# Buffers of the front, and the order of the step behind an out block, in a gated mix of two attention branches

## The chip, the cores and the metric

The kernel runs on one core of one Trainium2 chip. The metric is the device time of one execution in microseconds (us). The core has five engines that run side by side and meet by semaphores: PE (TensorE, the matmuls), DVE (VectorE), ACT (ScalarE), POOL (GpSimd) and SP (SyncE, which here only issues DMAs). Each engine takes its instructions strictly in the order of the program, so an instruction that waits holds up all behind it on that engine. PE's results land in PSUM, of which there are eight banks of 128 x 512 floats.

## The reference, cut to what matters

The input x has 2048 rows of 512. Two attention branches of 32 heads of 16 are computed from it and mixed row by row by a gate.

```python
# branch A: each query sees 8 keys, at distances 0, 2, ..., 14 behind it
qkv = x @ wqkv;  logits = einsum("bhsd,bhswd->bhsw", q, kg) * scale
o_a = einsum("bhsw,bhswd->bhsd", softmax(logits), vg);  a = o_a @ wo_a
# branch B: 32 query heads, one key head and one value head, all 2048 keys
q = x @ wq;  k = x @ wk;  v = x @ wv
o_b = einsum("bhqk,bkd->bhqd", softmax(q k^T * scale), v);  b = o_b @ wo_b
g = sigmoid((x * gate_w).sum(-1, keepdims=True))
return g * a + (1 - g) * b
```

Products that feed the softmax or the output are made from two parts (a rounded part and the rest), three matmuls for one, so that float precision is kept.

## The kernel before, in words

**Two phases.** The front makes all projections; the main loop computes branch B and, beside it on POOL, branch A. A planner written in Python runs while the program is built. It keeps estimated clocks of PE, ACT and DVE (`clk`) and times at which each PSUM bank becomes free (`free`), and from these it decides which instruction comes next. What it decides is fixed in the program: on the chip each engine follows that order and waits where the estimate was short.

**The front** (`front_stream`, up to about 285 us). PE computes 14 query projections and then 64 projections for branch A ("lumps"), each of 12 products with 64-row halves of the array, into four banks `pf` in turn. ACT copies each finished bank away.

- A query lump is copied to `qraw` (`queries_post`, line 223). POOL then rounds it to `qhi` and takes the rest as `qlo` (lines 230 and 231), and SP stores both in DRAM. There is one `qraw`, so the copy of a query waits until POOL has ended line 231 for the query before it.
- A lump of branch A is copied to one half of `stage` (`a_post`, line 257); after every second lump SP stores the buffer in DRAM (`ad`, line 265). There are two such buffers, used in turn, so a copy into a buffer waits until the store of two pairs earlier has landed. SP issues these stores in one queue with the query stores and with rows of eight small transfers each (`qst` from `ml`, line 459).

**Fills.** Branch B's softmax needs the largest score of each query. It comes from 2048 extra score matmuls ("fills") with 62-row halves, which the planner puts wherever PE has room: single ones into bank `ps` or `po` (line 328, DVE reduces 128 x 512, line 362), pairs into the two banks `pm` (DVE reduces 128 x 1024, line 350), or as differences: the difference of two key blocks goes to a bank `pd` (line 399), ACT applies Relu and copies it to `dd` (line 411), a second fill and one DVE operation (line 423) give the maximum of both.

**The main loop** has 512 steps, 16 tiles of keys for each of 32 units of queries. A step s has two score pairs, `exp_pair(s, 0)` and `exp_pair(s, 1)` (PE line 471, into the double banks `e0` and `e1`, named `pe` in the profile), each followed by one exponential on ACT (line 477, 128 x 1024), and `weighted(s - 1)`, eight matmuls of the values with the exponentials of the step before into bank `po` (line 486). Between them stand "m2" (a pair of fills into `pm`, if the bank is free within a slack) and "m1" (a single fill into `ps`).

**Out blocks.** Three times, at the first step of a unit, the step is an out block (`out_phase`, `stream`): the output rows of four tiles are computed by 96 products (line 803), each as an upper and a lower half. It uses `e0` and `e1` in turn; `pm` is given up and becomes the two difference banks `pd`. Near its end the planner calls the block "closing" and starts no more differences; once the scores of pair 0 are issued and both `pd` are free it makes `pm` out of them again (`rejoin`) and issues `exp_pair(s, 1)` into `pm`. The last result is taken from `e1` by ACT (line 685) and, behind it, DVE (line 686). The position of the first two blocks is fixed by a step number; the third comes at the first unit's end at which the fills are less than `LEAD` = 1.75 units ahead. The step behind a block has an order of its own. In the order of the step before the change,

```python
        if s - 1 in led:
            order = (0, "m2", "m1", "po", 1)
```

"po" is `weighted(s - 1)`, which needs bank `po` empty of the block's last fill, and both exponentials of the block's step.

**POOL** is busy with branch A (`a_scores`, `a_values`), in its own order; there `av` (line 605) is a scratch tile and `tr4` (line 554) another of the same size.

Of the kernel before, what the change touches and what calls it, by code (L numbers as in the profile page):

```python
# [6 lines left out]
F32 = mybir.dt.float32  # L7
# [6 lines left out]
P = 128  # L14
# [3 lines left out]
DH = 16  # L18
NJ = S // P
C = D // P  # L20
# [9 lines left out]
AG = 2  # L30
# [10 lines left out]
NH = NJ // 2  # L41
LEAD, M2S, M1S, MARGIN = 1.75, 0.5, 0.3, 0.12
# [6 lines left out]
def gated_mix_kernel(ctx, tc, xt, wa, wk, wq, wo_a, wo_b, out):  # L49
# [48 lines left out]
    dd2 = p1.tile([P, 2, 512], F32, name="dd2")  # L98
    wqh = p0.tile([P, C, D], F32R, name="wqh")
    wql = p0.tile([P, C, D], F32R, name="wql")  # L100
    wkr = p0.tile([P, C, P], F32, name="wkr")
    wqr = [t[:, k].rearrange("p (c q) -> p c q", c=C) for t in (wq01, dd) for k in range(2)]
    waraw, wah, wal = {}, {}, {}
    GO = [0, GN + VN, 2 * GN + VN, 3 * GN + VN]
# [112 lines left out]
    def queries_post(m, bank, key, ups_at):  # L217

        nonlocal pool
        settle("rest", 0)  # L220
        own = p0q.tile([P, 512], F32, name="qraw", bufs=1)
        hi, lo = parts_of()
        got = nc.scalar.activation(own, bank, AF.Copy)
        at = after("act", clk["pe"] + T_LAT, 0.62)
        mark(got, at, ups_at)
        free[key] = at + 0.1

        def rest():
            nonlocal pool
            nc.gpsimd.tensor_copy(hi, own)  # L230
            nc.gpsimd.tensor_sub(lo, own, hi.bitcast(F32))
            pool = max(pool, 1e3 * at) + 2300
            queries_out(m, hi, lo)
            if m > 4 and m % 2 and len(stacked) < NB:
                stack(len(stacked))

        tasks.append((max(pool / 1e3, at), rest, (), "rest"))
# [8 lines left out]
    def a_post(gg, j, bank, key, ups_at):  # L246

        if j % 2 == 0:
            settle("store", 1)
            if len(stages) < 2 or "next" in stage:  # L250
                stages.append((stage.pop("next", None) or p1).tile([P, GC, 2, AN], F32, name=f"stage{len(stages)}"))
            stage["t"] = stages[turns[1] % len(stages)]
            turns[1] += 1
        st = stage["t"]
        end = gg == C - 1 and j == NJ - 1
        src = bank[:, :GN].rearrange("p (g n) -> p g n", g=GC)
        got = nc.vector.tensor_copy(st[:, :, 1, :], src) if end else nc.scalar.activation(st[:, :, j % 2, :], src, AF.Copy)
        if gg == 0:
            nc.scalar.activation(vst[:, j, 0:DH + 1], bank[:, GN:GN + DH + 1], AF.Copy)
        at = after("dve" if end else "act", clk["pe"] + T_LAT, 0.5 if gg else 0.7)  # L260
        mark(got, at, ups_at)
        free[key] = at + 0.1
        if j % 2 == 1:
            dst = ad[gg * GC:(gg + 1) * GC, HALO:, :].rearrange("g (p j) n -> p g (j n)", j=NJ)
            tasks.append((at + 0.3, lambda: nc.sync.dma_start(dst[:, :, (j - 1) * AN:(j + 1) * AN], st.rearrange("p g j n -> p g (j n)")), (), "store"))
        if j == NJ - 1:
            tasks.append((at + 1.0, whole, (gg,)))
# [327 lines left out]
    def a_values(g, hf):  # L595
        lg, e = alog.pop(g), aext.pop(g)
        js = slice(NH * hf, NH * hf + NH)
        lgv = lg.rearrange("p w j h -> p w (j h)")
        nc.gpsimd.tensor_mul(asum[g], asum[g], gate[:, 0, js].unsqueeze(2).to_broadcast([P, NH, AG]))
        nc.gpsimd.tensor_mul(lgv, lgv, asum.pop(g).rearrange("p j h -> p (j h)").unsqueeze(1).to_broadcast([P, W, NH * AG]))  # L600
        yield 850
        ao = oa[g // 8][:, js, g % 8 * AC:(g % 8 + 1) * AC].rearrange("p j (h d) -> p j h d", d=DH)
        for w in range(W):
            o = HALO - DIL * w
            av = p2[0].tile([P, NH, AG, DH], F32, name="av", bufs=1) if w else ao
            nc.gpsimd.tensor_mul(av, e[:, o:o + NH, 2 * AC:].rearrange("p j (h d) -> p j h d", d=DH), lg[:, w].unsqueeze(3).to_broadcast([P, NH, AG, DH]))  # L606
            yield 730
            if w:
                nc.gpsimd.tensor_add(ao, ao, av)  # L609
                yield 830  # L610
# [130 lines left out]
    def stream(seq, mm, done, s):  # L741

        nonlocal pp2
        at, told = [0, 0], 0
        ready = free.pop("m2")
        pp2.release()
        pp2 = tc.alloc_tile_pool(name="parts", bufs=1, space=PSUM)
        if len(held[0]) < 2:
            more = p1x[0].tile([P, 2, 512], F32, name="dd2", tag="qx", bufs=1)
            for b in range(2):  # L750
                held[b].append(more[:, b])
                read_d[b].append(0.0)
        apart[:] = [pp2.tile([P, 512], F32, name=f"pd{k}") for k in range(2)]
        free["d0"] = free["d1"] = ready
        free["po"] = 1e9
        cl = [clk["pe"]] * 2
        while min(at) < len(seq) or any(pend):
            if free["po"] > 1e8 and min(at) > 3 and max(cl) > exped[s - 1] + 0.1:
                clk["pe"] = max(cl)
                weighted(s - 1)  # L760
                finish_a((s - 1) // NJ, nc.gpsimd)
                free["po"] = clk["dve"] + 0.1
                cl = [clk["pe"]] * 2
            if apart and max(at) > len(seq) - 6 and s in exped and max(free["d0"], free["d1"]) <= max(cl):
                clk["pe"] = max(cl)
                rejoin()
                exp_pair(s, 1, m2, "m2")
                cl = [clk["pe"]] * 2
            b = int(cl[1] < cl[0])
            clk["pe"] = cl[b]  # L770
            do = side_fill(b, max(at) > len(seq) - 6)
            if do:
                do()
                cl[b] += T_R
            elif at[b] < len(seq) and at[b] <= at[1 - b] + 2:
                dur = mm(b, seq[at[b]])
                cl[b] = clk["pe"] + dur
                at[b] += 1
            else:
                cl[b] += 0.07  # L780
            clk["pe"] = cl[b]
            while told < min(at):
                told += 1
                done(seq[told - 1])
        plain_todo()
        clk["pe"] = max(cl)
        if apart:
            rejoin()
            exp_pair(s, 1, m2, "m2")
# [469 lines left out]
    for s in range(NS + 1):  # L1259
        u, kt = divmod(s, NJ)  # L1260
        if len(stacked) < NU and s >= max(2, 16 * (gone(len(stacked)) + 1)):
            stack(len(stacked))
        if s < NS and kt == 0 and u not in shifted:
            while u not in shifted:
                clk["pe"] += 0.5
                run_tasks()
                if u not in shifted and left.get(u, 1):
                    assert pause(4)
        v = min(x[0][0] for x in (half, slots, [(NU,)]) if x)
        need = left.get(v, NF // NU)  # L1270
        steps = 16 * v - 6 - s
        short = need - 2.8 * max(0, steps) if v < NU else 0
        lead = (NF - to_go()) / 64 - s / 16
        order = (0, "m2", "m1", 1) if s > 1 else (1, "m2", "m1", 0) if s else ()
        if s - 1 in led:
            order = (0, "m2", "m1", "po", 1)
        k, n = outs // 4, C - (outs >= NJ - 4)
        if outs == NJ - 4:
            if short > 0 and steps < 2:
                pause(short)  # L1280
        elif due or outs < NJ and outs // NH in done and kt == 15 and NHG * (k + 1) - 1 in shaped and (lead < LEAD or s >= 16 * (NHG * (k + 2) + 1) - 1):
            if not due:
                prepare(outs, n)
                due.append(n)
            else:
                out_phase(list(range(outs, outs + 4)), due.pop(), s)
                outs += 4
                led.add(s)
                order = ()
        elif short > 0 and steps < 2:  # L1290
            pause(short)

        for which in order:
            if which == "m2":
                if slots or half:
                    fill_ready("m2", M2S)
                else:
                    next(tail, None)
            elif which == "m1":
                if singles(s) and fill_ready("m1", M1S):  # L1300
                    owing[0] -= 1.0
            elif which == "po":
                weighted(s - 1)
            elif s < NS:
                exp_pair(s, which)
        if s - 1 in exped:
            weighted(s - 1)
            if kt == 0 and s < NS:
                finish_a(u - 1, nc.gpsimd)
        run_tasks()  # L1310
        run_pool()
# [79 lines left out]
```

## Time and profile before

| | us |
|---|---|
| median of 3 runs | 1464.12 (1463.6 to 1466.82) |
| the profiled execution | 1463.92 |
| its span, first to last instruction | 1462.1 |
| PE busy in the span | 1448.2 (99%) |
| ACT busy | 1292.0 (88%) |
| DVE busy | 1141.9 (78%) |
| POOL busy | 954.6 (65%) |

The profiled execution is 1.8 us longer than its span; that rest lies outside the first and last instruction. In the rows of the timeline the first number is the start in us from the span's start, the second the duration; then engine, line, operation, what it writes and reads, and how many follow each other (xN). Square brackets hold the idle time of that engine just before, and whose end ended it. In a row of waits the three numbers are us in total, times, and the longest. In a row of windows stand the stretch, its length, the busy time of each engine with the number of its instructions, and PEclk, the share of full clock that TensorE was granted. Line numbers are those of the kernel before.

### The profile page before, as it was taken

Reading aid. Unit: us, or ns where it says so; the run is one execution under the profiler, and the core shown is the slowest. Engines: PE = TensorE matmul, PEld = TensorE weight load, DVE = VectorE, ACT = ScalarE, POOL = GpSimd, SP = SyncE. Lnnn points to the kernel's source line nnn. Section 1 sums busy time; section 2 is a strip of 40 time slices with the busy share of each in tenths; the row PEclk is TensorE's granted clock in tenths of the full one; section 3 lists DMA queues with packets and bytes.
Section 4 is the critical chain, followed back from the end, with each engine's and each line's share of the span. In section 5 each row is a group of like instructions: output and inputs, shape, how many; then the busy total and the mean of one; then the engine's idle time right before and its main releaser. Section 6 shows DMA issues by size and latency. Waiting matters only on the chain.

```text
span 1462.1 us, 29622 instructions
## 1 busy us (share of the span) xinstructions
PE 1448.2 (99%) x10989; PEld 743.1 (51%) x10989; DVE 1141.9 (78%) x1857; ACT 1292.0 (88%) x1649; POOL 954.6 (65%) x1714
## 2 busy tenths in 40 slices
PE   9999999999999999999999999999999999999999
PEld 6899999833333333333333373333333743373335
DVE  6888888788887888888888876888888778778821
ACT  5788888699999999999999988999999889879994
POOL 6951888888979898898898897888881211130000
PEclk9999999999999999999999999999999999999999
DMA  6652442411202111012022020211200000000000
GB/s 225 171 159 72 146 129 89 136 49 41 79 12 79 47 44 68 31 39 78 17 74 72 13 93 8 82 42 42 71 12 13 27 16 1 2 31 1 1 2 29
DMA packets 45688, 85.70 MB, mean 59 GB/s; under 512 B 10400, under 2 KB 28248, under 8 KB 41448
## 3 DMA queue, kind: packets, MB, share of 16 engines
q1 hardware_dynamic: 38552, 45.21, 10.0%
q0 software_dynamic: 6560, 37.95, 7.8%
q8 instruction: 86, 1.41, 0.4%
q10 hardware_dynamic: 432, 0.66, 0.1%
q14 instruction: 58, 0.48, 0.1%
HBM read 57.97 MB, written 25.25 MB: 57 GB/s over the span
## 4 chain that ended last, share of the span: by engine, by line
PE 92%; POOL 2%; ACT 2%; DVE 1%; issue 1%; DMA 1%; SPq 0%; POOLq 0%; ACTq 0%; DVEq 0%
PE po L486 34%; PE pe L471 24%; PE pf L1109 9%; PE pm L328 8%; PE ps L328 5%; PE pe L803 5%; PE pd L399 3%; PE po L328 1%; PE pe L1320 1%; ACT pexp L477 1%; DMA ad<-stage 1%; POOL xl L82 1%; DVE mx L350 1%; DMA xraw<-xt 0%; PE pf L195 0%
## 5 line engine op out<-in xcount | busy, mean ns | idle before, releaser
L477 ACT ACTIVATE pexp<-pe 128x1024 f32<-128x1024 f32 x1021 | 983.4, 1023 | 64.4 <-PE pe L471 61.1
L350 DVE TENSOR_REDUCE mx<-pm 128x2 f32<-128x1024 f32 x470 | 574.0, 1221 | 178.1 <-PE pm L328 174.4
L486 PE MATMUL po<-pexp,vst 128*32 128x512 f32 x4096 | 546.4, 605 | 4.5 <-DVE mx L423 3.3
L471 PE MATMUL pe<-qst,kst 64*128 64x512 f32 x1914 | 492.6, 459 | 2.0 <-ACT pexp L477 2.0
L471 PEld LDWEIGHTS pe<-qst,kst 64*128 64x128 f32 x1914 | 193.5, 184 | 437.0 <-ACT pexp L477 408.6
L411 ACT ACTIVATE dd<-pd 128x512 f32<-128x512 f32 x384 | 224.5, 601 | 50.7 <-PE pd L399 24.7
L362 DVE TENSOR_REDUCE mx<-ps 128x1 f32<-128x512 f32 x309 | 209.8, 679 | 3.4 <-PE pe L803 2.0
L328 PE MATMUL ps<-kst,qst 62*128 62x512 f32 x475 | 194.2, 409 | 0.2
L549 POOL TENSOR_TENSOR pr<-aext 128x256 f32<-128x256 f32 x256 | 181.9, 740 | 4.2 <-DMA aext<-ad 4.0
L328 PE MATMUL pm<-kst,qst 62*128 62x512 f32 x880 | 178.7, 397 | 0.5 <-ACT pexp L477 0.2
L609 POOL TENSOR_TENSOR oa<-oa,av 128x256 f32<-128x256 f32 x224 | 164.1, 733 | 15.8
L486 PEld LDWEIGHTS po<-pexp,vst 128*32 128x32 f32 x4096 | 80.6, 108 | 171.7 <-issue 157.2
L423 DVE CUSTOM_DVE_ANT_0 dd<-ps,dd 128x512 f32<-128x512 f32 x193 | 133.0, 689 | 25.8 <-PE ps L328 7.8
L423 DVE CUSTOM_DVE_ANT_0 dd<-po,dd 128x512 f32<-128x512 f32 x191 | 131.6, 689 | 22.6 <-PE po L328 10.2
L1109 PE MATMUL pf<-wal,xh 64*128 64x384 f32 (+1 forms) x496 | 148.3, 337 | 0.0
L399 PE MATMUL pd<-kd,qst 62*128 62x512 f32 x372 | 146.4, 398 | 1.7 <-ACT dd L411 1.7
L606 POOL TENSOR_TENSOR av<-aext,lg 128x256 f32<-128x256 f32 x224 | 139.4, 622 | 12.6
L1109 PE MATMUL pf<-wah,xh 64*128 64x384 f32 (+1 forms) x496 | 145.7, 338 | 0.0
L1109 PE MATMUL pf<-wah,xl 64*128 64x384 f32 (+1 forms) x496 | 142.3, 337 | 0.0
L328 PEld LDWEIGHTS ps<-kst,qst 62*128 62x128 f32 x475 | 87.8, 185 | 33.7 <-DVE mx L362 25.6
L513 POOL TENSOR_TENSOR rl<-rl,gate_t 128x16 f32<-128x16 f32 x31 | 7.1, 230 | 143.3 <-DVE rl L506 143.1
L1109 PEld LDWEIGHTS pf<-wal,xh 64*128 64x128 f32 x496 | 90.7, 186 | 0.3
(210 smaller groups left out, 1817.6 us busy)
## 6 DMA issues: line engine op xcount, KB each, us to landing
aext<-ad POOLq DMA_DIRECT2D x32, 1056.0 KB, 5.4
ad<-stage SPq DMA_DIRECT2D x32, 384.0 KB
qst<-qd SPq DMA_DIRECT2D x60, 128.0 KB
xraw<-xt SPq DMA_DIRECT2D x16, 256.0 KB
qd<-qhi SPq DMA_DIRECT2D x16, 256.0 KB
qd<-qlo SPq DMA_DIRECT2D x16, 256.0 KB
qst<-qd SPq DMA_DIRECT2D x60, 64.0 KB
qst<-ml SPq DMA_DIRECT2D x212, 2.0 KB
```

The costliest lines, as they stand in the source:

```text
L328: nc.tensor.matmul(dst, qst[place(v)][b:b + 62, pr, t * P:(t + 1) * P], kst[b:b + 62, kc * 512:(kc + 1) * 512], start=True, stop=True)
L350: got = nc.vector.tensor_reduce(m[:, :, pr, t, kc], dst, AX.X, ALU.max)
L362: got = nc.vector.tensor_reduce(m[:, odd, pr, t, kc:kc + 1], dst, AX.X, ALU.max)
L399: nc.tensor.matmul(dst, qst[place(v)][b:b + 62, pr, t * P:(t + 1) * P], kd[0][b:b + 62, kc // 2, :], start=True, stop=True)
L411: got = nc.scalar.activation(held[b][k], dst, AF.Relu)
L423: got = nc.vector.tensor_tensor_reduce(held[b][k], dst, held[b][k], 1.0, -FMAX, ALU.add, ALU.max, m[:, b, pr, t, kc:kc + 1])
L471: nc.tensor.matmul(bank[:, odd, :], kst[b:b + 64, kt * P:(kt + 1) * P], qst[place(u)][b:b + 64, pr, :], start=True, stop=True)
L477: got = nc.scalar.activation(e, bank, AF.Exp, scale=SCALE)
L486: nc.tensor.matmul(po[32 * i:32 * i + 32, :], vst[:, kt, :], pexp[s, i // 2][:, i % 2, :], start=(kt == 0), stop=(kt == NJ - 1))
L549: nc.gpsimd.tensor_mul(pr[:, k], q, e[:, o:o + NH, AC:2 * AC])
L609: nc.gpsimd.tensor_add(ao, ao, av)
L1109: inst = nc.tensor.matmul(home(x)[0][:, :n], l[h], r[h], start=(i == 0 and b == 0), stop=(i == 3 * C - 1 and b == 1))
```

## The change: what it does

It has four parts.

1. **Query copies.** A second buffer for the copies of even queries, `qraw2`, in the place of `wkr` (the weights of the keys, read for the last time before the first of these copies); odd queries keep `qraw`.
2. **Output buffers of the front.** Three buffers `stage` in place of two. To make room for them, `av` shares the memory of `tr4`; both are used by POOL alone.
3. **Closing.** A block is closing when more than 86 of its 96 products are issued on either half (`len(seq) - 10`), not 90 (`len(seq) - 6`). So its differences end four products sooner, and `rejoin` can come four products sooner.
4. **The step behind a block.** Its order becomes pair 0, m1, pair 1, m2, `weighted`; before it was pair 0, m2, m1, `weighted`, pair 1. The slack of m2 is 1.2 us there and not 0.5.

```diff
-    wkr = p0.tile([P, C, P], F32, name="wkr")
+    wkr = p0.tile([P, C, P], F32, name="wkr", tag="wkr", bufs=1)
...
-        own = p0q.tile([P, 512], F32, name="qraw", bufs=1)
+        own = p0q.tile([P, 512], F32, name="qraw", bufs=1) if m % 2 else p0.tile([P, 512], F32, name="qraw2", tag="wkr", bufs=1)
...
-            if len(stages) < 2 or "next" in stage:
+            if len(stages) < 3:
                 stages.append((stage.pop("next", None) or p1).tile([P, GC, 2, AN], F32, name=f"stage{len(stages)}"))
...
-            av = p2[0].tile([P, NH, AG, DH], F32, name="av", bufs=1) if w else ao
+            av = p2[0].tile([P, NH, AG, DH], F32, name="av", tag="tr4", bufs=1) if w else ao
...
-            if apart and max(at) > len(seq) - 6 and s in exped and max(free["d0"], free["d1"]) <= max(cl):
+            if apart and max(at) > len(seq) - 10 and s in exped and max(free["d0"], free["d1"]) <= max(cl):
                 clk["pe"] = max(cl)
                 rejoin()
                 exp_pair(s, 1, m2, "m2")
                 cl = [clk["pe"]] * 2
             b = int(cl[1] < cl[0])
             clk["pe"] = cl[b]
-            do = side_fill(b, max(at) > len(seq) - 6)
+            do = side_fill(b, max(at) > len(seq) - 10)
...
         if s - 1 in led:
-            order = (0, "m2", "m1", "po", 1)
+            order = (0, "m1", 1, "m2", "po")
...
-                    fill_ready("m2", M2S)
+                    fill_ready("m2", 1.2 if s - 1 in led else M2S)
```

## The prediction

> **What bounds the kernel now.** I read the page first. Its first part gives the busy time of the engines, its fourth the chain of work that ended last.
>
> ```profile
> span 1462.1 us, 29622 instructions
> ...
> PE 1448.2 (99%) x10989; PEld 743.1 (51%) x10989; DVE 1141.9 (78%) x1857; ACT 1292.0 (88%) x1649; POOL 954.6 (65%) x1714
> ...
> PE 92%; POOL 2%; ACT 2%; DVE 1%; issue 1%; DMA 1%; SPq 0%; POOLq 0%; ACTq 0%; DVEq 0%
> ```
>
> PE is the bound almost everywhere, and the change takes no matmul away. So it can save only time in which PE stood still (1462.1 - 1448.2 = 13.9 us) or ran slowly. The view of waits for PE says where it stood behind another engine, and one row of the windows shows how little of that lies in the steady main loop:
>
> ```profile
> PE po L486 <- DVE mx L423: 3.3, 2, 2.2
> PE pe L471 <- ACT pexp L477: 2.0, 5, 0.4
> PE pd L399 <- ACT dd L411: 1.7, 4, 0.9
> ...
> PE po L486 <- ACT pexp L477: 1.2, 1, 1.2
> ```
>
> ```profile
> 300.00:350.00 50.00, 50.00 (x357) 18.46 (x355) 40.45 (x47) 46.98 (x52) 44.25 (x89) 1.00 0.17 58
> ```
>
> In that stretch PE is busy for 50.00 of 50.00 us. The four wait rows add up to 3.3 + 2.0 + 1.7 + 1.2 = 8.2 us, and the timelines below put nearly all of it into the front and the few us behind the three out blocks, the places that the change touches.
>
> **Part 1, query copies.** ACT waits for the buffer of the query before (waits of ACT, up to 300 us), and soon after three of these four waits PE waits for ACT (timeline of PE):
>
> ```profile
> ACT qraw L223 <- POOL qlo L231: 4.4, 4, 2.5
> ```
>
> ```profile
> 39.22 0.39 PE L328 MATMUL po<-kst,qst 62*128 62x512 f32 x1
> 39.94 0.50 PE L399 MATMUL pd<-kd,qst 62*128 62x512 f32 x1 [0.33 <-ACT dd L411]
> ...
> 48.58 0.49 PE L399 MATMUL pd<-kd,qst 62*128 62x512 f32 x1 [0.16 <-ACT dd L411]
> ...
> 62.81 0.50 PE L399 MATMUL pd<-kd,qst 62*128 62x512 f32 x1 [0.33 <-ACT dd L411]
> ```
>
> The releaser is line 411, but that copy stands behind the delayed line 223 on ACT. The idle time is 0.33 + 0.16 + 0.33 = 0.82 us. A restart costs a little more: the first two starts are 0.72 us apart, where starts in a full stream are about 0.23 apart (876.60 and 876.84 below), a loss of 0.49, which is 0.16 above the idle time shown. With that for all three the loss is 0.82 + 0.48 = 1.30 us. Two buffers let ACT be one query ahead of POOL. POOL is no faster for it, but nothing on PE waits for POOL here. I take **1.30 us**; 0.82 is the low end.
>
> **Part 2, stage buffers.** Two copies wait for a store. From the whole chain in order of time, and the timelines of ACT and PE:
>
> ```profile
> 102.93 3.23 DMA ad<-stage
> 277.64 6.82 DMA ad<-stage
> ```
>
> ```profile
> 106.27 0.49 ACT L257 ACTIVATE stage<-pf 128x384 f32<-128x384 f32 x1 [1.52 <-DMA ad<-stage]
> ...
> 284.56 0.49 ACT L257 ACTIVATE stage<-ps 128x384 f32<-128x384 f32 x1 [3.01 <-DMA ad<-stage]
> ```
>
> ```profile
> 106.13 0.34 PE L1109 MATMUL pf<-wah,xl 64*128 64x402 f32 x1
> 107.37 0.49 PE L399 MATMUL pd<-kd,qst 62*128 62x512 f32 x1 [0.91 <-ACT dd L411]
> ...
> 286.02 0.50 PE L471 MATMUL pe<-qst,kst 64*128 64x512 f32 x2 [0.42 <-ACT pexp L477]
> ```
>
> The first store is issued late because SP works off other transfers before it, and lands at 106.16; the fifth lump needs that buffer. With a third buffer the fifth lump goes elsewhere, and the next use of the first is two lumps later, after the landing. PE's starts are 1.24 us apart, less some 0.2 of ordinary spacing: **1.05 us** (0.91 at least). The second wait is at the end of the front. PE worked on beside it, and stood only when it needed the exponentials queued on ACT behind that copy: I take those **0.42 us**, with 0 as the low end. The shared memory of `av` and `tr4` costs nothing: POOL alone writes and reads both, one after the other. The instructions of the front and their order stay as they are. Front: 1.30 + 1.05 + 0.42 = **2.8 us**, low end 0.82 + 0.91 = 1.7.
>
> **Parts 3 and 4, behind the blocks.** Block 1, from the timelines of PE, ACT, DVE and a window:
>
> ```profile
> 876.60 0.40 PE L471 MATMUL pe<-qst,kst 64*128 64x512 f32 x2
> ...
> 876.84 0.39 PE L399 MATMUL pd<-kd,qst 62*128 62x512 f32 x1
> ...
> 878.91 0.42 PE L471 MATMUL pm<-qst,kst 64*128 64x512 f32 x2
> 879.13 0.39 PE L803 MATMUL pe<-woh,qst 64*128 64x512 f32 x1
> ...
> 882.42 1.94 PE L486 MATMUL po<-pexp,vst 128*32 128x512 f32 x8 [2.25 <-DVE mx L423]
> 884.28 1.22 PE L471 MATMUL pe<-qst,kst 64*128 64x512 f32 x4
> ```
>
> ```profile
> 879.43 1.03 ACT L477 ACTIVATE pexp<-pm 128x1024 f32<-128x1024 f32 x1 [0.82 <-PE pm L471]
> 880.35 0.59 ACT L685 ACTIVATE two<-pe 128x512 f32<-128x512 f32 x1
> ```
>
> ```profile
> 880.97 0.69 DVE L686 COPY two<-pe 128x512 f32<-128x512 f32 x1 [1.36 <-ACT two L685]
> 881.58 0.68 DVE L423 CUSTOM_DVE_ANT_0 dd<-po,dd 128x512 f32<-128x512 f32 x1
> ```
>
> ```profile
> 883.00:884.00 1.00, 1.00 (x8) 0.00 (x0) 0.00 (x0) 0.00 (x0) 0.94 (x6) 0.50 0.20 59
> ```
>
> Read it backwards. `weighted` waits 2.25 us for line 423, which empties `po`; that stands on DVE behind line 686, which waits for ACT's line 685, which stands behind the exponential from `pm`, whose scores came last in the block because a difference (876.84) still held `pd`. Then TensorE's granted clock is 0.50: the eight matmuls take 1.94 us and the four after them 1.22. Blocks 2 and 3, timeline of PE, with the fourth gap of block 1 first:
>
> ```profile
> 886.19 0.49 PE L471 MATMUL pe<-qst,kst 64*128 64x512 f32 x2 [0.43 <-ACT pexp L477]
> ...
> 1177.96 1.06 PE L486 MATMUL po<-pexp,vst 128*32 128x512 f32 x8 [1.18 <-ACT pexp L477]
> 1178.96 0.73 PE L471 MATMUL pe<-qst,kst 64*128 64x512 f32 x4
> ...
> 1180.57 0.50 PE L471 MATMUL pe<-qst,kst 64*128 64x512 f32 x2 [0.42 <-ACT pexp L477]
> ...
> 1308.67 0.49 PE L328 MATMUL pm<-kst,qst 62*128 62x512 f32 x2 [0.22 <-ACT pexp L477]
> ...
> 1310.49 1.07 PE L486 MATMUL po<-pexp,vst 128*32 128x512 f32 x8 [1.10 <-DVE mx L423]
> ...
> 1313.11 0.49 PE L471 MATMUL pe<-qst,kst 64*128 64x512 f32 x2 [0.39 <-ACT pexp L477]
> ```
>
> Loss of block 1: 2.25 + 0.43 idle, and (1.94 - 1.06) + (1.22 - 0.73) = 1.37 by the clock: 4.05 us. Block 2: 1.18 + 0.42 = 1.60. Block 3: 0.22 + 1.10 + 0.39 = 1.71. Together 7.36 us; more isn't there to be won.
>
> The new order puts pair 1 ahead of `weighted`. Its scores go to `e1`, so PE now waits for lines 685 and 686 alone. With closing four products sooner the difference at 876.84 is not started, so the scores into `pm` can follow those of 876.60 (after well under the 2.3 us of now), and ACT has done both exponentials when the last product ends. What is late next is the chain from that product: a hop of 0.1, 0.59 on ACT, 0.69 on DVE (the copy starts 0.03 after ACT's end), a hop of 0.1: 1.5 us. Beside it PE has pair 0 (0.49, as at 1180.57) and the single fill of m1 (one spacing, 0.23): it stands 1.5 - 0.7 = 0.8 us. Behind that nothing waits: `pm` has been empty for long, and so has `po`, whose last difference went earlier. So each block keeps 0.8 us of its loss, and the gains are 3.25, 0.8 and 0.9: **4.9 us**. Low end: nothing comes earlier on ACT, and only the order changes; then block 1 stands until the copy's end at 881.66 instead of 882.42, escapes the half clock perhaps, and blocks 2 and 3 gain nothing: 0.76 to 0.76 + 1.37 + 0.43 = 2.6. High end: 7.36.
>
> The fills left out of the closing stretch (two to four matmuls in each block) are made up in later steps at 0.12 to 0.24 us each; the block is shorter by as much, and the step behind blocks 1 and 2 gains a pair in m2. I cost this at 0, with 1 us either way.
>
> The granted clock is 0.50 after an idle of 2.25 us, and after 1.18 and 1.10 us the eight matmuls ran at full speed (1.06, 1.07); 0.8 us should be safe. The Trainium skill, "TensorE: Matmul & The Clock Gate", section "What's actually happening", has the clock fall to half after at least one idle window of about 3.4 us, in windows that run free of the kernel. By that rule a gap of 2.25 us need not be the cause, and 1.37 us of the gain would be chance; the trace has the drop right behind the gap, so the measurement decides.
>
> **Sum.** 2.8 + 4.9 = 7.7 us off the profiled execution's 1463.92: **1456.2 us**. The median, 1464.12, is 0.2 above that execution, so it is the same forecast within what a measurement tells apart (about 0.2%, 2.9 us).
>
> **Rivals.**
> - *Only the order acts*: the planner's clocks let `rejoin` come no sooner, so ACT's line 685 stays behind the exponential from `pm`. Blocks give up to 2.6 us: 1463.9 - 2.8 - 2.6 = 1458.5. For it: block 2's row shows no wait for DVE, its `pm` scores came after all else. Against it: the diff changes the very condition, and `pd` is free as soon as ACT has copied the difference before.
> - *The front gives nothing*: the next thing binds at once, for instance POOL, busy 47.19 of 58 us from 34 to 92:
>
> ```profile
> 34.00:92.00 58.00, 56.94 (x488) 50.12 (x486) 48.67 (x142) 46.36 (x87) 47.19 (x57) 1.00 0.60 168
> ```
>
>   Then 1463.9 - 4.9 = 1459.0. Against it: PE lost 58.00 - 56.94 = 1.06 us there, nearly all in the three waits above.
> - *The clock falls behind every block*: the wait for `e1` leaves PE idle long enough for half clock each time. Each block then loses 0.8 + 1.37 = 2.2, together 6.5, against 7.36 before: 1463.9 - 2.8 - 0.9 = 1460.2. The skill's free-running window speaks for some chance of it, the two short gaps without a drop against it.
> - *Slower: the steady steps lose their cover.* The steps behind block 1 are planned anew. In each step the load of the score weights waits for the exponential:
>
> ```profile
> PEld pe L471 <- ACT pexp L477: 435.7, 550, 1.2
> ```
>
>   On average 435.7 / 550 = 0.79 us, hidden under `weighted` (1.06). If the new order leaves ACT in a later phase by more than the 0.27 us of cover, each of some 240 steps after block 1 shows PE idle. From 7.7 / 240 = 0.032 us per step the gain is gone; at 0.05 the time is 1456.2 + 12 = 1468.2. Against it: the front, two blocks and their different starts all fell back into steps without idle time.
>
> **Chances.** Forecast 0.62 (own range 1454 to 1459); only the order 0.13; no gain in front 0.08; half clock everywhere 0.09; slower steps 0.08. The range must leave out no more than 0.2: from all gains at their high ends, 1463.9 - 3.0 - 7.4 = 1453.5, rounded down by part of the fills' 1 us to 1453, up to 1461, which takes in the three middle cases. Faster by over 0.2% (under 1461.2): the first three and most of the fourth, 0.82. Within 0.2%: 0.10. Slower: 0.08.
>
> **What would show it.** Right: no wait of line 223 for line 231 and none of line 257 for `ad`; three gaps of about 0.8 us behind the blocks, released by DVE's line 686; granted clock 1.00 behind block 1; line 685 starting 0.1 us after the last product. Wrong: ACT's line 685 still behind the exponential from `pm`; `weighted` or pair 1 waiting over 1.5 us; a PEclk below 1 in those windows; PE idle in the steady rows; the front's end not 2 to 3 us sooner; or the third block in another unit, which would draw the whole end anew.

## The result, and the profile after

Median of four runs each: 1463.86 us before (1463.25 to 1466.82), 1457.77 us after (1457.52 to 1458.42). The ratio is 0.9951 with a 95% interval of 0.994 to 0.9963. That is 6.1 us by the medians and 5.5 by the two profiled executions (1463.92 and 1458.42, the latter the slowest of its four); 7.7 us were predicted. The page of the changed kernel, its first part and its chain:

```profile
span 1456.3 us, 29598 instructions
...
PE 1447.1 (99%) x10989; PEld 742.7 (51%) x10989; DVE 1146.2 (79%) x1853; ACT 1289.3 (89%) x1643; POOL 954.1 (66%) x1714
...
PE 95%; POOL 2%; DVE 1%; ACT 1%; issue 0%; DMA 0%; POOLq 0%; ACTq 0%; DVEq 0%
```

PE has the same 10989 matmuls and stands for 1456.3 - 1447.1 = 9.2 us, where it was 13.9. All waits of PE that the view lists:

```profile
PE pe L471 <- DVE two L686: 3.1, 3, 1.1
PE ps L161 <- POOL ident masks.py:199: 1.4, 1, 1.4
PE pm L328 <- DVE mx L350: 0.4, 1, 0.4
PE pe L471 <- ACT pexp L477: 0.3, 1, 0.3
```

The waits for lines 411 and 423 are gone. Three new ones stand in their place, one behind each out block, and a single one of 0.4. The windows shown of before, after the change:

```profile
34.00:92.00 58.00, 57.92 (x505) 51.72 (x503) 50.31 (x145) 47.12 (x90) 48.81 (x58) 1.00 0.60 169
300.00:350.00 50.00, 49.62 (x354) 18.37 (x351) 39.98 (x46) 46.69 (x51) 42.94 (x87) 1.00 0.19 63
883.00:884.00 1.00, 1.00 (x11) 0.16 (x8) 1.00 (x2) 1.00 (x2) 0.92 (x2) 1.00 0.00 0
```

PE's idle time from 34 to 92 us fell from 1.06 to 0.08, and the clock behind block 1 is 1.00, as in every window of 2 us of this execution. But from 300 to 350, where PE had been busy for all 50.00 us, 0.38 is now idle.

To see where the time came from, take from PE's two timelines the start of `weighted` (the row of line 486) at the same steps and subtract. "Ahead of" a block is the last `weighted` before its first product, "third after" the third behind its last:

| at | before | after | lead of after |
|---|---|---|---|
| step 0 (the front is done) | 286.45 | 283.70 | 2.75 |
| step 9 | 305.32 | 302.59 | 2.73 |
| step 12 | 311.81 | 309.49 | 2.32 |
| ahead of block 1 | 844.31 | 842.06 | 2.25 |
| third after it | 888.75 | 883.21 | 5.54 |
| ahead of block 2 | 1142.80 | 1137.87 | 4.93 |
| third after it | 1183.14 | 1177.45 | 5.69 |
| ahead of block 3 | 1273.88 | 1268.34 | 5.54 |
| third after it | 1315.43 | 1308.87 | 6.56 |
| last step | 1439.47 | 1433.76 | 5.71 |

Front and blocks gave 2.75 + 3.29 + 0.76 + 1.02 = 7.82 us. The stretches between them, which the prediction had at no change, took 0.50 + 0.61 + 0.15 + 0.85 = 2.11 back.

The gap that is left behind block 1, from PE's timeline, with those of blocks 2 and 3 below it:

```profile
875.78 1.11 PE L803 MATMUL pe<-woh,qst 64*128 64x512 f32 x8
876.72 0.40 PE L471 MATMUL pe<-qst,kst 64*128 64x512 f32 x2
876.96 0.40 PE L328 MATMUL ps<-kst,qst 62*128 62x512 f32 x1
878.36 0.50 PE L471 MATMUL pe<-qst,kst 64*128 64x512 f32 x2 [1.00 <-DVE two L686]
878.69 0.40 PE L328 MATMUL pm<-kst,qst 62*128 62x512 f32 x2
879.02 1.07 PE L486 MATMUL po<-pexp,vst 128*32 128x512 f32 x8
...
1172.62 0.50 PE L471 MATMUL pe<-qst,kst 64*128 64x512 f32 x2 [1.10 <-DVE two L686]
...
1304.05 0.49 PE L471 MATMUL pe<-qst,kst 64*128 64x512 f32 x2 [1.00 <-DVE two L686]
```

The chain beside it, on ACT and on DVE:

```profile
876.98 0.60 ACT L685 ACTIVATE two<-pe 128x512 f32<-128x512 f32 x1 [0.41 <-POOL tr L555]
```

```profile
877.61 0.69 DVE L686 COPY two<-pe 128x512 f32<-128x512 f32 x1 [1.02 <-ACT two L685]
```

The last product ends at 875.78 + 1.11 = 876.89. Line 685 starts 0.09 later, line 686 at 877.61, it ends at 878.30, and pair 1 starts at 878.36: 1.47 us, of 1.5 predicted. In blocks 2 and 3 the same stretch is 1.47 us too (1171.15 to 1172.62, 1302.58 to 1304.05). `weighted` runs in 1.07.

The wait in the steady rows, on DVE and on PE:

```profile
303.07 0.26 DVE L583 RECIPROCAL asum<-asum 128x16 f32<-128x16 f32 x1 [1.49 <-POOL asum L593]
303.24 1.17 DVE L350 TENSOR_REDUCE mx<-pm 128x2 f32<-128x1024 f32 x1
```

```profile
304.46 0.50 PE L328 MATMUL pm<-kst,qstx 62*128 62x512 f32 x2 [0.38 <-DVE mx L350]
```

Line 583 is a small operation of branch A and needs a sum from POOL. DVE takes its work in order, so the maximum that empties `pm` (line 350) stands behind it, and the next pair of fills behind that. POOL's sum and DVE's wait for it, before the change and POOL's after it:

```profile
305.13 0.22 POOL L593 TENSOR_TENSOR asum<-half 128x16 f32<-128x16 f32 x1
```

```profile
305.39 0.25 DVE L583 RECIPROCAL asum<-asum 128x16 f32<-128x16 f32 x1 [1.09 <-POOL asum L593]
```

```profile
302.82 0.22 POOL L593 TENSOR_TENSOR asum<-half 128x16 f32<-128x16 f32 x1
```

DVE waited before as well, 1.09 us that PE didn't feel. POOL came 2.31 us sooner and PE 2.73; the wait grew by 0.40, and PE's lead fell by 0.41.

The fills in two stretches of steps (line 328 alone), from block 1 to block 2 and from block 3 to the last step, before and after:

```profile
888.75:1142.80 254.05, 67.55 (x317) 1.00 0.12 38
1315.43:1439.47 124.04, 21.12 (x98) 1.00 0.01 1
```

```profile
883.21:1137.87 254.66, 67.83 (x319) 1.00 0.12 38
1308.87:1433.76 124.89, 22.02 (x102) 1.00 0.01 1
```

Six fills more stand in the steps (2 and 4), and the two stretches are 0.61 + 0.85 = 1.46 us longer, 0.24 us for each fill if that is all that lengthens them (the runs below bear on this). They replace the six differences that the blocks no longer make, by the groups of tile `pd`:

```profile
L399 PE MATMUL pd<-kd,qst x372: 386/394/498, 33.9 to 1305.1; 62*128 62x512 f32 x186
```

```profile
L399 PE MATMUL pd<-kd,qst x366: 387/394/499, 34.9 to 1298.3; 62*128 62x512 f32 x183
```

### The profile page after: what moved, and what is told of

Same layout as the page of the kernel before. It is cut to its first block, busy times and chain, and to the rows that moved or that the text cites. A ratio compares the mean times of both kernels' runs of the same rounds, so it can differ in the third digit from the quotient of the medians.

```text
span 1456.3 us, 29598 instructions
## 1 busy us (share of the span) xinstructions
PE 1447.1 (99%) x10989; PEld 742.7 (51%) x10989; DVE 1146.2 (79%) x1853; ACT 1289.3 (89%) x1643; POOL 954.1 (66%) x1714
## 3 DMA queue, kind: packets, MB, share of 16 engines
q8 instruction: 86, 1.41, 0.4%
## 4 chain that ended last, share of the span: by engine, by line
PE 95%; POOL 2%; DVE 1%; ACT 1%; issue 0%; DMA 0%; POOLq 0%; ACTq 0%; DVEq 0%
PE po L486 33%; PE pe L471 24%; PE pf L1109 11%; PE pm L328 8%; PE ps L328 6%; PE pe L803 4%; PE pd L399 3%; PE po L328 2%; PE pf L195 1%; PE pe L1320 1%; DVE mx L350 1%; ACT pexp L477 1%; POOL pr L549 1%; POOL tr L555 1%; PE pm L861 0%
## 5 line engine op out<-in xcount | busy, mean ns | idle before, releaser
L411 ACT ACTIVATE dd<-pd 128x512 f32<-128x512 f32 x378 | 221.2, 602 | 51.6 <-PE pd L399 26.6
L1109 PEld LDWEIGHTS pf<-wah,xl 64*128 64x128 f32 x496 | 90.6, 186 | 0.6
```

What stands on the lines that cost most here:

```text
L411: got = nc.scalar.activation(held[b][k], dst, AF.Relu)
L1109: inst = nc.tensor.matmul(home(x)[0][:, :n], l[h], r[h], start=(i == 0 and b == 0), stop=(i == 3 * C - 1 and b == 1))
```

## The experiments

The theory after the result: the gains are those of the prediction, and the missing 2 us are the six fills, the sum of POOL at 303 us, and gaps of 1.0 in place of 0.8. The rivals: the front's lead is lost to something else; the new order of the step isn't what gains; the clock decides. Each ratio is against executions of the kernel before that were taken beside the run.

**front_only**: parts 1 and 2 of the change; against the changed kernel (shortened; the same 6 stands in the condition of `rejoin`, and m2 has its slack of before)

```diff
-            do = side_fill(b, max(at) > len(seq) - 10)
+            do = side_fill(b, max(at) > len(seq) - 6)
...
-            order = (0, "m1", 1, "m2", "po")
+            order = (0, "m2", "m1", "po", 1)
```

> Parts 1 and 2 alone (second query buffer, third stage buffer); blocks as before. Theory (gains add up): the front ends 2.75 us sooner as in the changed kernel, about 0.4 of it is lost again at about 305 us where DVE waits for POOL, so 2.3 us: 1461.6, with the three gaps behind the blocks as before (2.25, 1.18, 1.10). Rival (POOL or a later stage swallows the front's lead): 1463.5 to 1464.

Measured: 1461.91 us, ratio 0.9973 (0.9962 to 0.9984). `weighted` of step 0 starts at 283.13, a lead of 3.32; 0.41 goes at step 10, and 2.74 are left ahead of block 1. Behind it 1.51 are left: the idle time there is 2.25 as before, but the half clock lasted longer (below). So the front's gain is real, and 1.2 us of it were hidden in this execution by the clock.

**blocks_only**: parts 3 and 4 (buffers as before).

> Parts 3 and 4 alone; the front as before. Theory: blocks gain 3.3 + 0.8 + 0.9 = 5.0 by the starts of the steps behind them, and 1.2 to 1.4 of that is given back in later steps where the fills are made up: 3.7 us, 1460.2. Rival (the half clock behind block 1 hung on the phase of its window and not on the gap): block 1 gains 1.4 less, 1461.6.

Measured: 1461.22 us, ratio 0.9971 (0.9962 to 0.9981). In the profiled execution step 0 starts 1.25 us later than before (0.4 of it a wait for the input at line 195), and block 1 turns a lead of -1.38 into 1.99, a gain of 3.37. The blocks' gain doesn't hang on the front.

**query_only**: part 1 alone, one execution.

> Part 1 alone on the kernel before. Theory: the three gaps of PE at 39, 48 and 62 us are gone (1.3 us), the two waits for the store stay (0.91 idle at 106; 0.42 at the front's end): the first weighted starts at 286.45 - 1.3 = 285.1, give or take the start's variation. Rival (POOL's copies bind at once): gaps move to later queries and 286.4 stays.

Measured: 1462.29 us; step 0 starts at 285.43, a lead of 1.02. The three gaps at 39, 48 and 62 us are gone, but PE's wait at the first store is 1.41 us where it was 0.91: of the 1.04 us won before it (PE runs out of work at 105.42, not at 106.46) 0.54 are left behind it (106.83, not 107.37). The store comes no sooner for it.

**stage_only**: part 2 alone, one execution.

> Part 2 of the change alone, three buffers for the front's output. By the prediction's terms the waits of line 257 for the stores go and the front ends 1.05 to 1.47 us sooner (first weighted product of step 0 at about 285.0 to 285.4, where it was 286.45), while the three short waits of PE for line 411 at 39, 48 and 62 us stay. Rival: the query copies' delay sets POOL's and SP's pace, so the stores land later too and the front gains under 0.6 us without part 1.

Measured: step 0 starts at 284.64, a lead of 1.81, more than the 1.05 to 1.47 of the prediction's terms; the three gaps stay. 1.02 + 1.81 = 2.83 is near the 2.75 of both together; each is from one execution, and the start alone varies by about 1 us (last section). The time, 1464.76, tells of something else: the clock, below.

**old_order**: parts 1 to 3; the step behind a block keeps its order and slack of before.

```diff
-            order = (0, "m1", 1, "m2", "po")
+            order = (0, "m2", "m1", "po", 1)
...
-                    fill_ready("m2", 1.2 if s - 1 in led else M2S)
+                    fill_ready("m2", M2S)
```

> The changed kernel with the old order of the step behind a block (part 4 undone, parts 1 to 3 kept). Theory: early closing empties po and pm before the block ends, so weighted fits into the 1.0 us in which the new order waits for e1; the three gaps shrink to 0.3 or less and the time is 1455 to 1457. Rival (the order is what gains): weighted waits again for DVE or for the exponential, and the time rises to 1459 to 1461.

Measured: 1456.19 us, ratio 0.9938 (0.9925 to 0.995), 1.5 us faster than the changed kernel. PE's timeline behind block 1:

```profile
876.31 0.40 PE L471 MATMUL pe<-qst,kst 64*128 64x512 f32 x2
876.54 0.40 PE L328 MATMUL pm<-kst,qst 62*128 62x512 f32 x2
876.78 0.39 PE L328 MATMUL ps<-kst,qst 62*128 62x512 f32 x1
877.10 1.07 PE L486 MATMUL po<-pexp,vst 128*32 128x512 f32 x8
878.10 0.74 PE L471 MATMUL pe<-qst,kst 64*128 64x512 f32 x4
879.09 0.49 PE L328 MATMUL pm<-kst,qst 62*128 62x512 f32 x2 [0.25 <-DVE mx L350]
```

Up to pair 1 no row has a bracket; the gap that is left, 0.25 us here and 0.33 and 0.23 behind blocks 2 and 3, is that of the next pair of fills, for line 350. With the early closing `po` and both exponentials are ready in time, so `weighted` fits into the 1.5 us of the copying, and pair 1 finds `e1` empty. The new order puts the one instruction that must wait ahead of the one that could fill the wait.

**late_close**: parts 1, 2 and 4; closing at `len(seq) - 6`.

> The changed kernel with the old closing (part 3 undone, parts 1, 2 and 4 kept). Theory: ACT's line 685 stands again behind the exponential from pm, so e1 comes 0.5 to 0.8 us later and PE stands 1.6 to 1.9 us behind blocks 1 and 3; the granted clock may fall in block 1: 1459.5, or 1461 with the half clock. Rival (closing sooner does nothing, the order is all): 1457.8.

Measured: 1458.0 us, ratio 0.995 (0.9938 to 0.9963): the changed kernel's time, where I had expected a loss. Block 1 does show it, on PE:

```profile
878.59 0.50 PE L471 MATMUL pe<-qst,kst 64*128 64x512 f32 x2 [1.58 <-DVE two L686]
878.93 0.40 PE L328 MATMUL pm<-kst,qst 62*128 62x512 f32 x2
879.26 1.49 PE L486 MATMUL po<-pexp,vst 128*32 128x512 f32 x8
```

PE stands 1.58 us, and by the clock the eight matmuls at 879.26 take 1.49 in place of 1.07 (behind blocks 2 and 3 it stands 1.10 and 0.38). By the starts of `weighted` its three blocks gain 0.81 - 1.13 + 0.97 = 0.65 us on those of before, the changed kernel's 5.07. But its blocks hold 216 fills and differences, the changed kernel's 201, and the fifteen needn't be made up: the steps from block 1 to the last win 0.16 + 1.41 + 1.19 = 2.76 us, where the changed kernel's lose 1.61. Two terms of 4.4 us cancel. So closing sooner isn't free: it moves fills from the blocks into the steps.

**old_order_fill**: old_order, and single fills (not differences) allowed while a block closes.

```diff
-        if todo[b] or paired() and len(todo[1 - b]) < 2:
+        if todo[b] or paired() and len(todo[1 - b]) < 2 and not closing:
...
-        elif slots and fillable() and single and not paired():
+        elif slots and fillable() and single and (closing or not paired()):
```

> The run old_order, and single fills allowed in the closing stretch (no differences). Theory (a fill beside the block's products takes half a slot, 0.12 us; in a step 0.26 to 0.31): three to four fills more per block, 10 in all, each 0.14 cheaper: 1.4 us off old_order, 1454.8. Rival (a fill costs the same in both places, and DVE's reductions now delay lines 686 and the emptying of po): 1456 to 1457.5.

Measured: 1455.71 us, ratio 0.9937 (0.9925 to 0.995). Only 0.5 below old_order and less than expected, and the two ranges overlap (1455.26 to 1456.26, 1455.73 to 1456.41). The planner placed few fills more in the blocks (42, 40 and 39, where old_order has 41, 38 and 38). They were no cheaper there: the blocks gain 3.70 + 0.42 + 1.45 = 5.57 us on those of before, old_order's 6.75, so 1.18 less, and the steps win 1.07 of it back. That is the rival of the expectation, a fill that costs the same in both places.

**after_again**: the changed kernel once more, beside the next runs.

> The changed kernel once more, beside the next two on one chip. 1457.8 again if the chip matters little; a front that ends 0.6 us earlier or later than 283.7 would show how much the start of the program varies from run to run.

Measured: 1457.68 us (1457.37 to 1458.22), ratio 0.9951 (0.9937 to 0.9964), 0.1 from the first median.

**old_order_sum**: old_order, and DVE's sum of branch A planned 2.0 us later behind POOL.

```diff
-                hooks.append((pool + 800, a_sum, g, ("sum", g, hf)))
+                hooks.append((pool + (2800 if pe else 800), a_sum, g, ("sum", g, hf)))
```

> The run old_order, and in the main loop DVE's reciprocal for branch A (line 583) is issued 2 us later by the planner's clock. Theory (the front's lead ran into DVE waiting for POOL at about 303): the stall of 0.38 us on PE is gone and the front's lead stays at its full size up to block 1: 0.4 us off old_order. Rival (the lead is lost to something else at the same place): same time as old_order. The plan behind changes too, which alone may move the time by 0.5.

Measured: 1455.06 us (1454.9 to 1455.19), ratio 0.9933 (0.992 to 0.9945): the fastest of all, 1.1 below old_order. The lead goes from 3.67 at step 9 to 3.88 at step 12; nothing is lost at 303 us.

**after_sum**: the same edit in the changed kernel.

> The changed kernel, with one number altered: DVE's sums of branch A (line 593) are planned 2.0 us later behind POOL's end than before. The theory: the front came 2.75 us sooner but POOL's sum only 2.31, so DVE stood 1.49 us for POOL at 303 us and PE lost 0.41 us there; without that wait the lead of the front stays whole at step 12, and the median is 0.4 to 1.2 us under the changed kernel's 1457.7 (1456.5 to 1457.3), about what the same edit gave beside the old order (1.1). The rival: what the old order gained by this edit was another drawing of the steps; then the wait goes but the time stays within 0.3 us of 1457.7.

Measured: 1457.16 us, ratio 0.9948 (0.9935 to 0.996), 0.5 to 0.6 below the changed kernel. On DVE at the same place:

```profile
303.14 0.24 DVE L583 RECIPROCAL asum<-asum 128x16 f32<-128x16 f32 x1
303.52 1.23 DVE L350 TENSOR_REDUCE mx<-pm 128x2 f32<-128x1024 f32 x1
```

The 1.49 us have gone, PE has no wait for line 350 left, and the lead rises from 3.57 at step 9 to 3.80 at step 12, where the changed kernel's fell by 0.41. The other runs agree: the eight that have a sooner front and the sum where it was lose 0.38 to 0.48 at step 10, and blocks_only, with the front of before, loses nothing there. The edit also draws later steps anew (the lead is 4.59 ahead of block 1 and falls by 1.28 between blocks 1 and 2), so the 0.5 to 0.6 is not the price of this wait alone.

**one_copy**: the changed kernel, but `e1` is emptied by one ACT copy (line 689) and not by lines 685 and 686.

```diff
-        if closing:
+        if closing and False:
```

> The changed kernel, but a block's last result is taken from e1 by one ACT copy of 128x1024 (1.02 us in nine rows of line 689) and not by ACT's 0.60 and, behind it, DVE's 0.69. The theory, that the gap behind a block is a chain from the last product to the end of that copying: the chain is 0.1 + 1.02 + 0.1 = 1.22 us and not 1.5, so each of the three gaps of PE is about 0.25 us shorter (0.75 to 0.85 in place of 1.00 to 1.10), released by ACT, and the time is 0.5 to 0.8 us lower (1457.0). The rival: ACT, 0.42 us longer at the copy, is late with the next exponentials, PE waits there for line 477 what it saves at e1, and the time stays at 1457.7 or rises by up to 0.5.

Measured: 1457.08 us, ratio 0.9948 (0.9936 to 0.9961), 0.6 to 0.7 below the changed kernel. PE's three rows:

```profile
877.38 0.50 PE L471 MATMUL pe<-qst,kst 64*128 64x512 f32 x2 [0.72 <-ACT two L689]
...
1171.39 0.50 PE L471 MATMUL pe<-qst,kst 64*128 64x512 f32 x2 [0.77 <-ACT two L689]
...
1302.70 0.50 PE L471 MATMUL pe<-qst,kst 64*128 64x512 f32 x2 [0.70 <-ACT two L689]
```

The gaps are 0.28 + 0.33 + 0.30 = 0.91 shorter, as the chain says. One copy of 1.02 us beats two of 0.60 and 0.69 that run one behind the other.

**old_order_both**: old_order with the later sums and the single fills.

> Parts 1 to 3 of the change with the step's old order, the later sums of branch A, and single fills allowed while a block closes. Each of the two edits alone was worth 1.1 and 0.5 us beside the old order (1456.19 to 1455.06 and 1455.71). If the two are independent terms: 1454.6. Rival: the planner draws the later steps anew with each edit and 0.5 is within that, then 1455.0 to 1455.6.

Measured: 1455.13 us, ratio 0.9935 (0.9921 to 0.9948). The same as old_order_sum; the 0.5 of the single fills doesn't add to it. Why not stays open; the planner draws all later steps anew with each such edit.

Closing and order in the four mixtures, all with the front of the change:

| | old order | new order |
|---|---|---|
| closing at 6 | 1461.91 (front_only) | 1458.0 (late_close) |
| closing at 10 | 1456.19 (old_order) | 1457.68 (after_again) |

Each edit alone gains, 5.7 and 3.9 us; both together gain 4.2, less than the closing alone. They are two cures for one wait. Part of all three gains is the half clock, which front_only had in each of its seven executions (mean granted clock 0.996 to 0.999) late_close in four of five, and the two kernels with the closing at 10 in none.

The fills in the steps, against those of the kernel before, and what the lead did over the same steps:

| | block 1 to block 2 | block 2 to block 3 | block 3 to the last step |
|---|---|---|---|
| query_only | 0 fills, +0.02 us | 0, -0.03 | 0, -0.01 |
| front_only | 0, +0.11 | 0, -0.09 | 0, +0.08 |
| the changed kernel | +2, -0.61 | 0, -0.15 | +4, -0.85 |
| old_order | +2, -0.62 | 0, -0.17 | +4, -0.85 |
| blocks_only | +2, -0.62 | 0, -0.10 | +4, -0.79 |
| old_order_fill | +1, -0.45 | -1, +0.22 | +2, -0.34 |
| late_close | 0, +0.16 | -5, +1.41 | -4, +1.19 |

Where the fills are the same, the lead moves by no more than 0.17 us; where they differ, it moves with them, by 0.17 to 0.45 us for each.

## Why the prediction was right or wrong

The time and the places were right; the gain was 1.6 us short by the medians and 2.2 by the profiled executions. By its steps:

- *Front 2.8.* 2.75 by step 0, and 3.26 and 3.32 in after_again and front_only. Of the single terms, the queries gave 1.02 alone and the buffers 1.81, where 1.30 and 1.47 had been taken. The sum held within the spread of the start, about 1 us; that it held to 0.05 is luck. PE's idle time from 34 to 92 us was not quite all in the three gaps (0.82 of 1.06): a wait of 0.23 for line 423 at 59.43 went with them.
- *"Nothing on PE waits for POOL here."* True in the front. It failed 20 us later: POOL's sum moved forward by 0.42 less than PE did, and PE lost 0.41. after_sum takes this wait away. The prediction had named a POOL-bound front as a rival and looked for it from 34 to 92 us alone.
- *Blocks 3.25, 0.8 and 0.9.* 3.29, 0.76 and 1.02. The gap has the predicted place, releaser and chain (1.47 of 1.5), but it is 1.00, 1.10 and 1.00 and not 0.8. The cover was counted wrongly: pair 0 starts at 876.72, ahead of the last product's end at 876.89, so PE has work until 876.96 + 0.40 = 877.36, 0.47 behind that end and not 0.7. So waits and clock fell from 7.36 to 3.10, by 4.26 us and not by 4.95. That the blocks are 5.07 shorter all the same leaves 0.81 us for the six differences that they no longer make; this is a subtraction, and that it makes up for the 0.7 lost in the gaps is luck.
- *"The fills left out ... I cost this at 0, with 1 us either way."* The blocks won 0.81 by them and the steps paid 1.46, so the term is -0.65 and not 0. It lies inside its bound; the price of 0.24 for a fill in a step stood in the prediction's own sentence as the upper end, while the shorter block was taken to make up for all of it. The price is an average: no run adds fills to steps and changes nothing else, but over the runs the lead moves with them.
- *What the new order does.* The prediction was right on what the step would wait for, but it gave the blocks' 4.9 to closing and order together. old_order shows that the closing alone gives as much, and that with it the new order costs 1.5 us.
- *The clock, 1.37.* It ran at 1.00 behind block 1, as forecast. The prediction counted the 1.37 as a gain and said that it might be chance; the runs show that it is a chance, below.

Against the prediction, then, the last step is 2.0 us later: 0.7 by the gaps, 0.65 by the fills, 0.4 by POOL's sum, and some 0.3 that no run places.

The forecast's rivals: *only the order acts* and *the front gives nothing* fell by the table of leads, *the clock falls behind every block* by the granted clock of 1.00, and *slower steps* by the waits of PE, where the steady steps show one, at 304 us. One sum of the chances is off: the first three cases alone make 0.83, and most of the fourth comes on top, where 0.82 stands for all of them; the forecast time doesn't use it.

## What to carry to other kernels

If an instruction must wait for a buffer, put behind the trigger of that wait the work that is ready and as long as the wait, and try such an order again after every edit that makes more work ready: two cures for one wait don't add up. Work that a planner is kept from placing in one stage isn't gone; count it and price it where it lands. And when one stage gets shorter, ask which engines moved forward by less: the first engine that takes its work in order and needs one of them gives the lead back.

## What the runs showed of the hardware

The half clock starts by chance and comes in lengths of about 3.4 us. In a window of 2 us, the time at half clock is what PEclk lacks to 1, divided by 0.5 and times 2 us. Part 2 alone, at block 3, first the wait on PE's timeline and then the windows:

```profile
1310.55 1.06 PE L486 MATMUL po<-pexp,vst 128*32 128x512 f32 x8 [1.09 <-DVE mx L423]
```

```profile
1310.00:1312.00 2.00, 1.45 (x12) 0.52 (x14) 2.00 (x4) 0.08 (x1) 2.00 (x3) 0.94 0.00 0
1312.00:1314.00 2.00, 2.00 (x9) 0.91 (x5) 1.17 (x2) 1.80 (x2) 1.45 (x3) 0.50 0.42 135
1314.00:1316.00 2.00, 2.00 (x14) 0.60 (x14) 0.88 (x2) 1.14 (x2) 0.00 (x0) 0.70 0.02 1
```

0.24 + 2.00 + 1.20 = 3.44 us. In the same way: 3.40 in the kernel before and 6.84 in front_only and stage_only, each behind an idle time of 2.25 us at block 1, and 3.40 in late_close behind 1.58. Part 1 alone has the same idle time of 2.25 and no drop, by PE's timeline:

```profile
881.95 1.06 PE L486 MATMUL po<-pexp,vst 128*32 128x512 f32 x8 [2.25 <-DVE mx L423]
882.95 0.73 PE L471 MATMUL pe<-qst,kst 64*128 64x512 f32 x4
```

So the same wait in the same place cost nothing, once 3.4 us, twice 6.8 us at half clock. Of the 21 gaps of 0.99 to 1.18 us behind blocks in nine traces, the 1.09 us above is the only one with a drop: short gaps aren't safe either, only less exposed. The Trainium skill, "TensorE: Matmul & The Clock Gate", section "What's actually happening", has windows of about 3.4 us that run free of the kernel. The lengths and the chance agree with that; its condition of at least one idle window doesn't, since no idle time here was over 2.25 us.

The price shows in the spread. The kernel before ran 33 times beside the experiments; by the mean granted clock of an execution:

| mean clock | executions | mean time, us |
|---|---|---|
| 1.000 | 11 | 1463.61 |
| 0.999 | 8 | 1464.68 |
| 0.998 | 8 | 1466.27 |
| 0.997 | 3 | 1466.50 |
| 0.996 | 3 | 1467.30 |

The changed kernel had 1.000 in all nine, from 1457.37 to 1458.42. So part of what the change gives is an end to that spread: beside undisturbed executions it gains 1463.61 - 1457.7 = 5.9 us, beside the others up to 9.6. The clock isn't the whole spread: one of the eleven took 1465.90 us, and blocks_only, at 1.000 in all nine executions, went from 1460.49 to 1463.11.

The start has a spread as well: ten profiled executions with the front of the change reached step 0 between 282.68 and 283.70, and the two with the front of before at 286.45 and 287.70, so a lead in one profiled execution is known to about 1 us, and only differences along one execution are finer.
